# A new issue order for one fused attention and channel-mix kernel: the first loads in another sequence, every engine's list written anew

## The chip, the cores and the metric

The kernel runs on one core of a Trainium2 chip. A core has engines that each work through their own list of instructions in order: TensorE (PE, with its weight loads shown as PEld), VectorE (DVE), ScalarE (ACT), GpSimd (POOL) and SyncE (SP). SP, ACT and POOL also issue DMAs; the transfers run on 16 DMA engines that the queues share. An engine goes on to its next instruction only when the semaphores that this one waits for have been reached, so one late input holds everything behind it on the same engine. The metric is the device time in microseconds of one execution, the median of several.

## The reference

Two layers in a row. First a linear attention over 8 batches, 8 heads, 576 positions, head size 64:

```python
q_s = exp(q - max(q, -1));  q_s = q_s / sum(q_s, -1)        # softmax over the head size
k_s = exp(k - max(k, 2));   k_s = k_s / sum(k_s, 2)         # softmax over the positions
kv  = einsum('bhsd,bhse->bhde', k_s, v)
x   = einsum('bhsd,bhde->bhse', q_s, kv)                    # then (B, S, H*D) = (8, 576, 512)
```

Then a channel mix with weights `w_k` (512 x 1024), `w_v` (1024 x 512) and `w_r` (512 x 512):

```python
x_prev = x shifted by one position, zero at the start of each batch
xk = mu_k * x + (1 - mu_k) * x_prev
xr = mu_r * x + (1 - mu_r) * x_prev
out = sigmoid(xr @ w_r) * (relu(xk @ w_k) ** 2 @ w_v)
```

## The kernel before

The kernel has no loops on the chip. `graph` (from L187) makes a list of named operations with what each must follow and which buffers it takes and gives back; `Plan.ordered` (L159) then walks through the string `ORDER` (L48 to L125) and emits them in that order. A word of `ORDER` is `name:places`: the operation, and the numbers of the buffers that its new slots get. `ACT!load00q0` puts a load on ACT's queue in place of its usual one. Each operation has one engine, so the string fixes five lists, one for each engine; between engines only the data and the buffers order the work. Buffer numbers are shown in the profile as letters: `raw` 0 to 10 are raw_a to raw_k, `th` 0 to 6 are th_a to th_g, `mm` 0 to 3 are the PSUM banks mm_a to mm_d, and two pairs of banks att_a and att_b.

**Attention.** Work goes by pairs of a batch b and a group g of four heads (16 pairs, tag `bg`). `loadbgq`, `loadbgk`, `loadbgv` (L211) fetch q, k and v of a pair into raw buffers; batch 0 goes by SP and ACT and, for v, by POOL, and everything else by POOL's queue, 288 KB a piece for batches 0 and 1 (two pieces a tensor, last digit 0 or 1) and 576 KB after that. On POOL's queue stand also the weights: `wk00`, `wk01`, `wk10`, `wk11` (wk_aa, wk_ab, wk_ba, wk_bb, 256 KB each as written), `wr` (512 KB), `wv0` to `wv3`. ACT makes `expq`, `expk` (L337) and `cast` (v to bf16, L343); DVE makes `rsum`, `rrec`, `scale` (L352 to L361). On PE, `TKV`, or a joint block `B` or `M`, transposes q and multiplies k and v (L376, L406); a `B` or `M` block also holds the product of q and kv of an earlier pair (L545), which needs that pair's `qt` (ACT copy, L384) and `w` (DVE, L423). Then ACT copies the result out of PSUM (`xb`, `xs`, L553 and L557) and DVE makes the two mixes with the neighbouring position: `edge`, `diff`, `sc`, `mix` (L566 to L580). `mixbg0` feeds xk, `mixbg1` feeds xr.

**Channel mix.** The 4608 rows are cut into ten units u (512 rows, every fifth 256; unit 0 is 512 rows of batch 0, unit 2 reaches into batches 1 and 2). For each unit: eight groups `kuf` of four matmuls 128x512 (L673), each followed by `relu` on ACT (L660) and a square `sq` on DVE (L664); for each tile m of 128 rows `rum`, four matmuls with `wr` (L709), and a tanh `thum` on ACT (L714); then `vum0` and `vum1`, eight matmuls (L729), and `oum` on DVE (L735), which multiplies tanh and result inside the th buffer. Two stores `stum` (L745, first half, and `stum.2`, second half; 128 KB each) bring it out, on SP's queue.

Three uses of buffers matter below:

- A bank mm that a `k` took is free after its `relu`, one that an `r` took after its `th`, one that a `v` took after its `o`.
- A th buffer is taken by a `th` (ACT writes it) and free again when both stores of the tile that had it before have landed.
- A raw buffer is free when the `exp` or `cast` that reads it is done; the load that takes it next stands on POOL's queue.

At the start PE runs 27 `fill` matmuls on a constant, whose results nobody reads.

Of the kernel before, what the change touches and what calls it, by code (L numbers as in the profile page):

```python
# [60 lines left out]
load11v0:9 relu01:0 X001:0.3 k06:1 x0010 load11v1 wv0 expq110:0 wv1 x0111 k04:0 x0011 expk100
sq01 wv2 rrec101 scale101 TKV10:1 rsum110:3 rz10:2 w10:0 relu06:2 sq00 expq111 sq06 k05:2
relu04:0 k07:3 qt10:2 relu07:1 relu05:2 r00:1 r01:0 r03:3 rsum111 rrec110 rrec111 expk111:0
expk110 r02:2 sq05 wv3 scale111:0 cast110:1 sq07 scale110 cast111 B11:0.1 rz11:0 w11:1
# [14 lines left out]
load51q0:10 TKV30:1 rsum310:3 rrec310 relu24:0 v111 rz30:0 st13.2 k23:1 load41k0:0 cast310:2
expk400:2 sq24:0 o11 w30:1 sc2111:1 load41q0:2 k27:0 sc2110 o12 relu23:2 k20:3 k26:2 qt30:2  # L80
cast400:0 relu27:1 k21:1 scale310:1 mix211 B31:0.1 st13 sq23 relu21:0 mix201 sq27 k22:0 rz31:1
sq21 relu20:2 xb30:1 relu22:1 st03 w31:2 st11.2 st11 r23:1 xs30 rsum400:0 sq20 rrec400 sq22
th23:6 qt31:3 scale400:2 r22:3 edge30 th22:3 relu26:0 r30:0 diff30:0 sq26 sc3011:0 sc3010 k25:1
B40:1.0 v220:3 relu25:2 xb31:0 xs31 v200:2 th30:4 sc3001:1 v230:1 sq25 load61k0:1 load50q0:9
sc3000 edge31 expk410:0 v231 cast510:1 mix300 diff31:1 sc3100:2 sc3101 rz40:2 v201 cast410:2
expq410:2 load61v0:4 o23 v221 st01 w40:0 mix310 k41:0 r21:1 st12 o20 o22 st22.2 relu41:1
expq510:1 k40:2 v210:0 rsum410:1 rrec410 k42:3 load71q0:0 th21:0 sq41:1 st23 load50v0:5 relu40:0
relu42:2 k46:1 sq40 relu46:1 sc3111:1 qt40:1 st22 k37:2 expq500:0 scale410:0 st20.2 k33:3 k44:1
v211 rsum510:2 sq46 relu37:0 sq42 sc3110 expk510:1 B41:0.1 mix301 sq37:0 k34:2 relu44:1
load50k0:7 rrec510 rz41:0 o21 load60q0:2 relu33:2 mix311 w41:1 k45:1 k43:3 expk500:2 sq33 sq44  # L90
rsum500:3 relu43:0 xs40:1 relu45:2 k30:0 sq45 sq43 relu34:1 xb40 st20 k47:3 rrec500 relu47:2
scale500:1 st10 edge40 r33:1 th33:3 sq47 r31:2 diff40:0 st12.2 scale510:2 st10.2 k31:3 th31:2
relu30:0 load71k0:10 cast500:0 st23.2 r41:1 v410:2 k35:0 v411 sc4011:2 load60v0:9 expq600:2
load71v0:3 load61q0:7 relu31:2 th41:5 rsum600:0 o41 r40:3 sq31 sc4010 qt41:0 th40:1 load70k0:5
k36:1 sq30 relu35:2 mix401 sc4000:0 rrec600 qt50:2 sq34 relu36:0 M5:1.1 st41.2 k32:0 cast600:2
relu32:1 r32:1 st41 rz51:1 rz50:2 sc4001 sq35 xb41:0 w50:2 w51:0 sq32 v400:0 xs41 mix400
cast610:0 th32:6 sq36 edge41 expk600:0 cast710:1 qt51:3 diff41:1 v401 v320:2 sc4110:1 v300:3
v321 sc4101:2 sc4100 v301 mix410 sc4111 o32 k51:1 st21.2 expk610:1 o30 k57:2 mix411 v330:3 v331
expk710:2 relu51:2 expq610:0 relu57:1 scale600:0 o33 v310:1 st33.2 o40 expq710:1 rsum610:1
rrec610 v311 expq700:2 st30.2 o31 M6:1.0.1 k54:0 rz61:0 rz60:2 st21 w61:1 sq57:1 k53:1 sq51  # L100
xb50:1 relu54:0 xs50 edge50 relu53:1 k52:0 relu52:2 k55:1 diff50:0 sq54 w60:0 qt60:1 relu55:0
r50:0 sq52 xs51:0 k50:1 rsum700:3 scale610:1 k56:2 relu50:2 r53:3 sq50 rrec700 sq53 th50:5 xb51
edge51 sc5001:0 sc5000 mix500 sc5011:2 diff51:1 r51:1 sq55 r52:0 th53:0 relu56:2 v500:3 sq56
v530:2 sc5100:1 st40.2 st30 v531 expk700:0 st32.2 sc5010 sc5101 mix510 st32 th51:4 th52:6 v520:1
v501 k60:0 o53 relu60:1 scale700:2 k61:2 relu61:0 qt61:0 st31.2 o50 sc5110:0 rsum710:2 st31
sq60:0 k65:0 sc5111 k63:3 load70v0:2 cast700:0 st53.2 qt70:2 relu63:2 mix501 sq61 v521 o52 sq63
M7:1.0.1 k62:1 rz70:1 rz71:0 relu65:1 k66:0 w71:2 w70:0 relu62:0 xb61:1 sq62 xs61 mix511 edge61
relu66:2 rrec710 sq66 xs60:0 diff61:0 v510:1 st50.2 sc6101:1 v511 xb60 k67:0 k64:2 relu67:0
relu64:2 edge60 sq67 o51 sq64 r61:3 r63:0 v610:2 th61:2 st33 sq65 diff60:1 r60:1 st52.2 sc6001:2
th60:3 st40 st52 scale710:0 qt71:3 sc6100 sc6000 th63:1 mix600 sc6010:0 sc6111:2 v600:3 v611  # L110
v601 o60 st60 r62:1 v620:0 sc6110 st60.2 mix610 th62:6 k76:3 st53 sc6011 o61 k71:1 relu71:0
mix601 v621 o62 sq71:1 st51 k77:2 k75:1 relu75:2 sq75 k72:0 relu77:1 sq77 relu72:0 sq72 k73:1
k70:2 relu73:2 v630:0 st62 relu76:1 mix611 r72:1 relu70:0 th72:3 M8:1.1.0 v631 xs70:0 xs71:1
xb71 xb70 k74:1 sq76 sq70 r73:2 r71:3 th71:0 relu74:1 sq73 o63 edge70 edge71 diff70:0 diff71:1
# [796 lines left out]
```

## Time and profile before

| | |
|---|---|
| median of 3 runs | 194.69 us (194.67 to 194.73) |
| the profiled execution: its own time | 195.4 us |
| its span, first to last instruction | 193.6 us |
| around the span (195.4 - 193.6) | 1.8 us |
| profiled execution against the median | 0.7 us longer |
| mean granted TensorE clock | 0.995 |
| HBM read and written | 33.56 MB and 9.44 MB |

How to read it: the page first gives each engine's busy time, then the span in 40 slices of 4.84 us, where a digit is the busy share in tenths. Further views are the timeline (start, duration, instruction), the same by stretches of time, the DMA issues with their time from issue to landing, and the chain of work that ended last. Rows of SP's and ACT's queues (SPq, ACTq) and of POOL's DMA instructions give the time of the issue, not of the transfer. On an engine that is never idle the next instruction starts a little before the row of the last one ends, so that the cost of an instruction in a row of such is the distance of two starts, a little below its duration.

### The profile page before, as it was taken

The page shows a single profiled execution, that of the slowest core. Times are in us where ns is not written, and L with a number is a line of the kernel's source. Part 1 is how long each engine was busy: PE and PEld are TensorE (multiplying, and loading weights), DVE is VectorE, ACT ScalarE, POOL GpSimd, SP SyncE. Part 2 cuts the span into 40 slices and gives each one's busy share as a digit, 9 for nine tenths or more (in the row PEclk, how much of TensorE's full clock was granted, in tenths as well). Part 3 has the DMA queues.
Part 4 walks back from the last instruction along what each step waited for, and adds up shares of the span by engine and source line. Part 5 has one row for each costly group of instructions (what it writes and reads, how often), then busy time and mean ns, then how long its engine had stood idle before and what let it go on. Part 6 is the DMA issues. An engine that isn't in the chain of part 4 may idle for free.

```text
span 193.6 us, 4674 instructions
## 1 busy us (share of the span) xinstructions
PE 184.6 (95%) x1830; PEld 89.6 (46%) x1830; DVE 154.6 (80%) x368; ACT 138.8 (72%) x226; POOL 41.3 (21%) x65
## 2 busy tenths in 40 slices
PE   7698889999999999999999999999999999999991
PEld 2263344444545544655454544454444445554450
DVE  1788965999999999999999899997986494661521
ACT  3688899899999999899999878258425742357010
POOL 8346457453415402421200000000000000000000
PEclk9999999999999999999999999999999999999997
DMA  5999999999999997999990294253065003720085
GB/s 187 311 314 283 298 329 247 404 390 416 398 393 390 406 412 268 317 359 413 284 290 3 50 201 83 62 123 78 0 136 116 3 0 81 166 51 5 11 204 164
DMA packets 23614, 41.86 MB, mean 216 GB/s; under 512 B 9372, under 2 KB 12712, under 8 KB 23592
## 3 DMA queue, kind: packets, MB, share of 16 engines
q0 software_dynamic: 9392, 27.99, 43.3%
...
HBM read 33.56 MB, written 9.44 MB: 222 GB/s over the span
## 4 chain that ended last, share of the span: by engine, by line
PE 84%; DMA 11%; POOL 2%; issue 0%; DVE 0%; POOLq 0%
PE mm_a L729 9%; PE mm_a L673 9%; PE mm_b L673 9%; PE mm_d L729 8%; PE mm_c L729 8%; PE mm_b L729 7%; DMA wk_ab<-in_moe_w_k_dram 6%; PE mm_c L673 6%; PE mm_b L709 6%; PE mm_d L673 5%; DMA wr<-in_moe_w_r_dram 5%; PE mm_d L709 4%; PE mm_a L709 4%; PE mm_c L709 3%; PE att_b L545 1%; PE att_a L545 1%
## 5 line engine op out<-in xcount | busy, mean ns | idle before, releaser
L729 PEld LDWEIGHTS <-k_a 128*128 128x128 bf16 x152 | 14.6, 98 | 15.6 <-issue 0.5
L729 PEld LDWEIGHTS <-k_b 128*128 128x128 bf16 x144 | 13.9, 98 | 16.4 <-issue 0.2
L709 PEld LDWEIGHTS <-xr 128*128 128x128 bf16 x144 | 13.7, 98 | 16.6 <-DMA wr<-in_moe_w_r_dram 0.6
L709 PE MATMUL mm_b<-wr,xr 128*128 128x512 bf16 x48 | 12.5, 379 | 0.1
L673 PEld LDWEIGHTS <-wk_aa 128*128 128x128 bf16 x80 | 7.5, 98 | 8.7 <-issue 1.3
L673 PEld LDWEIGHTS <-wk_bb 128*128 128x128 bf16 x80 | 7.8, 98 | 7.7 <-DMA wk_bb<-in_moe_w_k_dram 0.2
L673 PEld LDWEIGHTS <-wk_ab 128*128 128x128 bf16 x80 | 7.7, 98 | 7.7 <-DMA wk_ab<-in_moe_w_k_dram 0.2
L673 PEld LDWEIGHTS <-wk_ba 128*128 128x128 bf16 x80 | 7.5, 98 | 8.2 <-issue 1.1
L709 PE MATMUL mm_d<-wr,xr 128*128 128x512 bf16 x36 | 9.2, 379 | 0.0
L664 DVE TENSOR_TENSOR k_b<-rel_b 128x512 bf16<-128x512 bf16 (+1 forms) x15 | 5.7, 381 | 4.4 <-ACT rel_b L660 4.2
L709 PE MATMUL mm_a<-wr,xr 128*128 128x512 bf16 x32 | 8.2, 379 | 0.0
L660 ACT ACTIVATE rel_a<-mm_b 128x512 bf16<-128x512 f32 (+1 forms) x8 | 4.7, 583 | 4.4 <-PE mm_b L673 2.3
L664 DVE TENSOR_TENSOR k_a<-rel_c 128x512 bf16<-128x512 bf16 (+1 forms) x14 | 5.6, 399 | 2.4 <-ACT rel_c L660 2.3
L660 ACT ACTIVATE rel_c<-mm_b 128x512 bf16<-128x512 f32 (+1 forms) x9 | 5.3, 590 | 3.0 <-PE mm_b L673 3.0
L673 PE MATMUL mm_b<-xk,wk_ab 128*128 128x512 bf16 x24 | 7.3, 379 | 0.0
L660 ACT ACTIVATE rel_b<-mm_a 128x512 bf16<-128x512 f32 (+1 forms) x7 | 4.2, 602 | 4.2 <-PE mm_a L673 4.2
L709 PE MATMUL mm_c<-wr,xr 128*128 128x512 bf16 x28 | 7.2, 379 | 0.0
L673 PE MATMUL mm_b<-xk,wk_aa 128*128 128x512 bf16 x24 | 7.2, 380 | 0.0
L664 DVE TENSOR_TENSOR k_a<-rel_a 128x512 bf16<-128x512 bf16 (+1 forms) x16 | 6.1, 384 | 1.2 <-ACT rel_a L660 1.2
L673 PE MATMUL mm_a<-xk,wk_ba 128*128 128x512 bf16 (+1 forms) x24 | 6.9, 370 | 0.0
L673 PE MATMUL mm_a<-xk,wk_bb 128*128 128x512 bf16 (+1 forms) x24 | 6.9, 370 | 0.0
L664 DVE TENSOR_TENSOR k_b<-rel_c 128x512 bf16<-128x512 bf16 (+1 forms) x14 | 5.4, 385 | 1.7 <-ACT rel_c L660 1.3
...
## 6 DMA issues: line engine op xcount, KB each, us to landing
raw_a<-in_q_dram POOLq DMA_DIRECT2D x3, 576.0 KB, 8.9
raw_c<-in_q_dram POOLq DMA_DIRECT2D x3, 576.0 KB, 9.7
raw_e<-in_v_dram POOLq DMA_DIRECT2D x3, 576.0 KB, 11.6
out_dram<-th_g SPq DMA_DIRECT2D x13, 128.0 KB, 2.4
out_dram<-th_d SPq DMA_DIRECT2D x12, 128.0 KB, 5.0
out_dram<-th_b SPq DMA_DIRECT2D x10, 128.0 KB, 4.2
out_dram<-th_a SPq DMA_DIRECT2D x10, 128.0 KB, 2.3
raw_b<-in_k_dram POOLq DMA_DIRECT2D x2, 576.0 KB, 10.9
```

The source lines that it names most:

```text
L545: kn.nc.tensor.matmul(kn.half(slot, u)[two[r], to:to + n], lhsT=kn.ws[w.index][two[u], r, :], rhs=x_columns(r, u, at, n), start=True, stop ...
L660: kn.nc.scalar.activation(out=kn.rels[rel.index][:, 0:n], in_=kn.bank(kf)[:, 0:n], func=ACT.Relu, scale=HALF_ROOT)
L664: kn.nc.vector.tensor_tensor(out=kn.k2s[k2.index][:, fc, 0:n], in0=kn.rels[rel.index][:, 0:n], in1=kn.rels[rel.index][:, 0:n], op=ALU.mult)
L673: kn.nc.tensor.matmul(kn.bank(kf)[:, 0:n], lhsT=kn.wk[fc // 4][ct % 2][:, ct // 2, (fc % 4) * 128: (fc % 4) * 128 + 128], rhs=kn.xs[0][:, ...
L709: kn.nc.tensor.matmul(kn.bank(rps), lhsT=kn.xs[1][:, ct, c:c + 128], rhs=kn.wr[:, ct, :], start=(ct == 0), stop=(ct == CT - 1))
L729: kn.nc.tensor.matmul(kn.bank(vps)[:, 0:width], lhsT=kn.k2s[k2.index][:, ft, 128 * m:128 * m + 128], rhs=wv_of(ft)[:, part], start=(ft == ...
```

## The change

Only `ORDER` differs. The set of operations (970 words) is the same, and so is every instruction's shape; the order and some buffer numbers change: 71 of the 76 lines are replaced by 70. PE's list is equal up to `fill.21 T01`; ACT's up to `x0000`, DVE's up to `kvn00`. The core of the diff:

```diff
 ACT!load00q0:0 zero ident load00q1 ACT!load00k0:1 load01q1:2 ACT!load01q0 rows load00v consts
-warm load00k1 load01v late load01k0:3 load10v1:4 wk00 load10q0:5 expq001:0 expq000 load10q1
-rsum001:0 ACT!load01k1 rsum000 wk01 expq011:1 rrec001 load10k1:6 rrec000 rsum011:1 fill:1
+warm load00k1 load01v late load01k0:3 load10q0:4 wk00 load10q1 expq001:0 expq000 load11q0:5
+rsum001:0 ACT!load01k1 rsum000 wk01 expq011:1 rrec001 load10k0:6 rrec000 rsum011:1 fill:1
...
-expk011 KV011 Z01 load10v0 wk11 qt01:1 rz01:1 edge01 kvn01:1 x0000 load11q0:7 load10k0 mu:2
+expk010:1 fill.19:3 fill.20:1 fill.21:1 T01:3 wk11 kvn00:0 edge00 wp000:0 fill.22:0 X000:1.0
+KV010:2 expk011 KV011 Z01 load10k1 wp001 qt01:1 x0001 load10v0:7 X001:0.3 load10v1 x0000 edge01
...
-load20v0:10 load20q0:0 load30q0:2 th01:0 load20k0:1 th02:1 v010:0 sq04 v000:2 th00:2 v030:1
+scale111 load30q0:10 cast110:1 expk110:0 load20v0:0 expk111 cast111 B11:1.0 rz11:0 load20q0:2
+sq04 w11:1 th03:0 th02:1 load20k0:1 sq05 th00:2 load21q0:3 v030:1 v010:0 xb10:0 v000:2 v031 xs10
...
-o00 st00.2 sc1101 mix1100 mix1101 v023 load30k0:8 o01 load40k0:9 k11:2 st03.2 k11.2 k11.3
...
-v100:1 scale300:0 th13:6 st01.2 th20:2 X21:0.1 xs21:1 xb21 sc2010:2 v120:2 expk300:0 th10:1
...
+load41v0:3 sq14 edge20 rrec300 qt21:1 scale300:0 expk300:0 r11:1 v120:0 th12:6 X21:1.0 v121
+cast400:1 v131 diff20:0 v100:2 v101 xb21:1 sc2011:2 xs21 st03 o12 o13 th11:1 sc2001:1 cast310:2
+edge21 cast300:0 v110:0 sc2000 diff21:1 sc2101:0 sc2100 st13 v111 mix200 o11 sc2010 expq310:2
+st11 st00.2 st00 expk310:1 r20:3 expq400:0 TKV30:1 load40k0:4 mix210 rz30:0 mix201 load41q0:6
+load60q0:8 o10 st10.2 k24:1 k21:0 load51k0:0 load70v0:5 k20:2 rsum310:3 st10 st13.2 st12.2 w30:1
+load71v0:7 rrec310 relu21:2 relu24:1 sq24:0 scale310:1 th20:2 load50v0:9 k23:0 k27:1 sc2111:1
+relu20:0 expk400:2 qt30:2 k25:3 sc2110 sq21 sq20 rsum400:0 k26:2 B31:0.1 relu26:1 relu25:2 k22:2
...
```

Taken apart by engine, the stretches that the prediction uses are these (before above, after below):

```
POOL  load00v load01v load10v1 wk00 load10q0 load10q1 wk01 load10k1 wk10 load10v0 wk11 load11q0 load10k0 load11q1 wr load11k1 load11k0 load11v0 load11v1 wv0 ..
      load00v load01v load10q0 wk00 load10q1 load11q0 wk01 load10k0 wk10 wk11 load10k1 load10v0 load10v1 load11q1 wr load11v0 load11k0 load11k1 load11v1 wv0 ..
POOL  .. wv3 load20v load20q load30q load20k load21q load21k load21v load60k load30v load30k load40k load31q load40q load31k load31v ..
      .. wv3 load30q load20v load20q load20k load21q load21k load21v load30v load31v load31q load30k load40q load40v load41k load31k ..
PE    .. X011 k01.2 X001 k06 k04 TKV10 k05 k07 r00 r01 r03 r02 B11 ..
      .. k02.2 X011 k07 k05 k06 k04 TKV10 r03 r02 r00 r01 B11 ..
PE    .. v110 k24 TKV30 v111 k23 k27 k20 k26 k21 B31 ..                (r20 earlier, after B21)
      .. v110 v111 r20 TKV30 k24 k21 k20 k23 k27 k25 k26 B31 ..
ACT   .. qt21 th13 th20 xs21 xb21 expk300 th10 cast300 expq310 expq400 expk310 relu24 cast310 expk400 relu23 qt30 ..
      .. qt21 expk300 th12 cast400 xb21 xs21 th11 cast310 cast300 expq310 expk310 expq400 relu21 relu24 th20 relu20 expk400 qt30 ..
SP    .. st00.2 st03.2 st00 st02.2 st02 st01.2 st13.2 st13 st03 st11.2 st11 st01 st12 ..
      .. st02 st02.2 st03 st13 st11 st00.2 st00 st10.2 st10 st13.2 st12.2 st01.2 st12 ..
DVE   edge10 diff10 sc1000 sc1001 sc1010 mix100 edge11 sc1011 diff110 diff111 o03 ..
      edge10 diff10 sc1000 sc1010 sc1001 sc1011 edge11 mix100 diff111 o01 diff110 sc1101 sc1100 sc1111 mix1100 mix1101 o03 ..
```

In both lists `th00` and `th20` have th buffer 2 (th_c), and in the new one `r20` and `k25` have bank 3 (mm_d), one after the other.

More of the change, by code (lines that the diff above doesn't have):

```diff
@@ L61 @@
[L61 to L64, printed above, removed]
-load20v0:10 load20q0:0 load30q0:2 th01:0 load20k0:1 th02:1 v010:0 sq04 v000:2 th00:2 v030:1
-xb10:0 v001 v031 xs10 v011 edge10 diff10:0 sc1000:0 sc1001 load21q0:3 qt11:3 th03:3 X11:1.0
@@ L67 @@
-xs11:1 xb111 v032 v002 load21k0:5 xb110 load21v0:4 v033 v020:3 v012 sc1010:1 mix100 edge11
-cast200:2 v003 v013 v021 sc1011 diff110:1 diff111 load60k0:6 load30v0:7 v022 o03 k13:1 sc1100:2
-o00 st00.2 sc1101 mix1100 mix1101 v023 load30k0:8 o01 load40k0:9 k11:2 st03.2 k11.2 k11.3
-sc1110:0 expq200:1 load31q0:10 expq300:2 o02 mix101 k13.2 sc1111 relu11:2 k15:0 sq11:1 rsum200:0
-k13.3 load40q0:0 k10:3 mix111 k10.2 expk200:1 k10.3 k17:2 relu15:1 k12:0 rrec200 k12.2 relu13:0
-sq15 expq210:0 k12.3 r12:1 relu10:2 load31k0:2 relu17:1 expk210:2 scale200:1 k16:3 st00
@@ L73 @@
-load31v0:1 sq13 rsum210:1 TKV20:0 load51k0:3 sq17 rz20:1 relu12:0 cast210:0 rrec210 relu16:1
-w20:2 r13:2 qt20:1 r11:0 st02.2 st02 scale210:2 k14:3 sq10 th11:4 relu14:2 sq12 th12:5 rsum300:2
-B21:1.0 r20:0 xs20:0 rz21:2 xb20 load51v0:5 w21:0 qt21:0 rrec300 sq14 edge20 sq16 diff20:0 r10:3
-v100:1 scale300:0 th13:6 st01.2 th20:2 X21:0.1 xs21:1 xb21 sc2010:2 v120:2 expk300:0 th10:1
-sc2000:1 edge21 sc2001 diff21:1 v130:0 cast300:1 sc2100:0 expq310:1 v131 v101 load40v0:4 sc2101
-mix200 expq400:0 expk310:1 o13 mix210 v110:3 v121 o10 sc2011 load70q0:8 load41v0:7 k24:0
@@ L79 @@
[L79 to L114, printed above, removed]
@@ new lines @@
+rz01:1 kvn01:1 wp010:1 mu:0 x0010 x0011 k01:1 X010:1.0 expq101:2 mucopy wp011 x0101 expq100
+x0100 rsum100:2 expk100:2 k00:2 k02:3 k03:0 k03.2 k01.2 relu01:0 rsum101 relu03:1 k00.2 load11q1
+wr rrec100 load11v0:8 sq01:0 scale100:2 load11k0:9 rrec101 sq03 k02.2 X011:0.1 x0111 relu00:2
+x0110 expq110:0 rsum110:3 k07:1 k05:0 load11k1 k06:2 sq00 relu02:0 expk101 cast100:0 cast101
+relu07:1 k04:3 scale101 sq07 TKV10:0 rz10:2 sq02 relu05:2 relu06:1 load11v1 expq111 wv0 wv1
+w10:0 r03:1 r02:0 wv2 r00:2 wv3 relu04:0 rrec110 scale110:0 rsum111 qt10:2 r01:3 rrec111 sq06
@@ new lines @@
+scale111 load30q0:10 cast110:1 expk110:0 load20v0:0 expk111 cast111 B11:1.0 rz11:0 load20q0:2
+sq04 w11:1 th03:0 th02:1 load20k0:1 sq05 th00:2 load21q0:3 v030:1 v010:0 xb10:0 v000:2 v031 xs10
+edge10 diff10:0 sc1000:0 sc1010:1 sc1001 v001 load21k0:4 v011 qt11:3 sc1011 X11:0.1 xs11:1
+th01:3 edge11 xb111 mix100 v012 load21v0:6 v013 load30v0:7 v002 v003 v020:3 xb110 diff111:1 o01
+diff110 sc1101:2 v032 expq300:1 load31v0:5 load31q0:9 sc1100 load30k0:8 v033 v021 v022
+load40q0:10 sc1111:0 k13:0 v023 mix1100 k13.2 mix1101 o03 k10:1 k13.3 o00 k12:2 cast200:2
@@ new lines @@
+expq200:2 k12.2 mix101 o02 load40v0:0 relu13:1 k10.2 load41k0:2 k10.3 rsum200:0 sq13:1 expk200:1
+k16:0 k12.3 k17:3 sc1110 relu10:0 rrec200 sq10 relu16:2 k14:1 k15:0 scale200:1 expq210:0
+relu17:1 mix111 relu14:0 sq16 k11:3 k11.2 expk210:2 rsum210:1 k11.3 relu11:2 sq11 TKV20:1
+load31k0:1 r13:1 rz20:1 cast210:0 rrec210 r10:3 w20:2 relu12:2 scale210:2 sq12 qt20:0 rsum300:2
+r12:2 th10:4 th13:5 st02 B21:0.1 v130:3 st02.2 relu15:2 rz21:2 sq15 w21:0 xb20:0 xs20 sq17
+load41v0:3 sq14 edge20 rrec300 qt21:1 scale300:0 expk300:0 r11:1 v120:0 th12:6 X21:1.0 v121
@@ new lines @@
+xs30:0 mix211 rz31:1 relu27:0 sq26 sq25 xb30 relu23:1 rrec400 w31:2 scale400:2 edge30 sq23 r22:3
+qt31:3 diff30:0 sq27 th22:4 relu22:2 st01.2 r23:1 th23:5 r30:0 B40:1.0 load61k0:1 xs31:1
+load50q0:10 load51q0:4 st12 xb31 r21:3 sq22 sc3000:0 th21:6 expk410:0 expq410:1 sc3001 expk510:1
+v230:2 v231 rz40:2 mix300 st03.2 v200:1 load51v0:2 edge31 diff31:1 th30:0 v220:3 sc3100:2 sc3101
+v201 o23 w40:0 load71q0:6 expq500:2 st11.2 mix310 k40:2 k46:0 relu46:1 relu40:0 rsum410:1 v221
+o20 sc3111:1 k41:0 sq46:1 relu41:2 sq40 k47:1 k42:2 relu47:1 sc3110 rrec410 o22 k36:0 k45:1
```

50 lines of the change are left out of this document (36 added, 14 removed).

## The prediction

> **What bounds the kernel now.** First the page: busy shares and slices.
>
> ```profile
> PE 184.6 (95%) x1830; PEld 89.6 (46%) x1830; DVE 154.6 (80%) x368; ACT 138.8 (72%) x226; POOL 41.3 (21%) x65
> ...
> PE   7698889999999999999999999999999999999991
> ```
>
> PE is full from its sixth slice of 4.84 us to the end, so the end is the time at which PE may start without gaps, plus its fixed work, plus any hole made in it later. Then the busy time by stretches:
>
> ```profile
> 20.00:25.00 5.00, 3.77 (x60) 1.68 (x60) 4.58 (x10) 4.29 (x9) 2.82 (x5) 1.00 1.15 303
> ...
> 35.00:60.00 25.00, 24.97 (x248) 11.47 (x245) 24.93 (x54) 23.49 (x33) 9.75 (x15) 1.00 1.04 399
> 60.00:75.00 15.00, 15.00 (x271) 7.55 (x270) 14.93 (x34) 15.00 (x23) 4.14 (x6) 1.00 1.04 403
> ...
> 100.00:130.00 30.00, 30.00 (x304) 14.07 (x303) 28.67 (x64) 22.62 (x36) 0.00 (x0) 1.00 0.43 93
> ```
>
> The second number of a row is PE's busy time, then PEld, DVE, ACT and POOL. From 35 to 75 us PE, DVE, ACT and the DMA engines (share 1.04) are all full at once. A wait on any of them there has no cover. After 100 us only PE is. Third, the chain of work that ended last, at its head:
>
> ```profile
> 5.35 12.36 DMA wk_ab<-in_moe_w_k_dram
> ...
> 18.00 9.29 DMA wr<-in_moe_w_r_dram
> ...
> 27.33 1.04 PE mm_b L709 x4
> ```
>
> The gapless part starts when `wr` has landed, at 18.00 + 9.29 = 27.29.
>
> **The first loads.** `wr` is the 15th load of POOL in both lists, and the same bytes stand ahead of it: four wk, two v of batch 0, eight pieces of pairs 10 and 11. Its issue followed the landing of the 7th (`wk01`, 5.35 + 12.36 = 17.71), which is the 7th again. So I take its landing as unchanged, 27.3. PE has the same groups ahead of the first `r` as before (`k04` to `k07` and `TKV10` among them), only with `TKV10` last; they need no more than before, and what PE saves of its holes (5.00 - 3.77 = 1.23 us between 20 and 25 us) is paid back by a longer wait for `wr`. This part: 0, bounds -0.3 (the wait for `wr` was already short) to +0.3.
>
> **Two small waits.** Cost of the new DVE order from 34.69:
>
> ```profile
> 34.69 0.84 DVE L575 TENSOR_SCALAR xm_a<-xd_a,mu 128x576 bf16<-128x576 bf16 x2
> 35.45 0.36 DVE L575 TENSOR_SCALAR xm_b<-xd_a,mu 128x576 bf16<-128x576 bf16 x1
> 35.72 0.75 DVE L580 TENSOR_TENSOR xk<-xm_a,xb_a 128x1152 bf16<-128x1152 bf16 x1
> 36.39 0.18 DVE L566 COPY xb_b<-xb_b 128x126 bf16<-128x126 bf16 x1
> 36.49 0.36 DVE L575 TENSOR_SCALAR xm_b<-xd_a,mu 128x576 bf16<-128x576 bf16 x1
> 36.77 0.81 DVE L570 TENSOR_TENSOR xd_b<-xb_b 128x576 bf16<-128x576 bf16 x2
> 37.51 0.67 DVE L735 SCALAR_TENSOR_TENSOR th_d<-th_d,mm_b 128x512 f32<-128x512 f32 x1
> 38.11 0.35 DVE L575 TENSOR_SCALAR xm_c<-xd_b,mu 128x576 bf16<-128x576 bf16 x1
> ...
> 39.27 0.81 DVE L580 TENSOR_TENSOR xk<-xm_c,xb_b 128x576 bf16<-128x576 bf16 x2
> 40.00 0.67 DVE L735 SCALAR_TENSOR_TENSOR th_a<-th_a,mm_a 128x512 f32<-128x512 f32 x1
> ```
>
> By the distances of starts, `o03` (the reader of mm_b) now has ahead of it four `sc` (0.76 + 0.27 + 0.28), `edge11` 0.10, `mix100` 0.67, two `diff` 0.74, `o01` 0.60, three `sc` 0.84 and two half mixes 0.73: it starts at 34.69 + 4.99 = 39.68 and ends at 40.35. `k10`, which takes mm_b, comes on PE right behind `k13 v023 k13.2`:
>
> ```profile
> 39.00 0.59 PE L673 MATMUL mm_b<-xk,wk_aa 128*128 128x512 bf16 x2
> ...
> 39.86 0.59 PE L673 MATMUL mm_c<-xk,wk_aa 128*128 128x512 bf16 x2
> ```
>
> that is at 39.86, where `k11` came before, plus one matmul, 0.22 (two take 39.86 - 39.00 less `v023`'s two, 0.43): 40.08. A wait of 0.3.
>
> Second, ACT now has `cast400` between `qt21` and `xb21`. Its tensor is the 13th load behind `wv3`; before, the 13th was this one into raw_a:
>
> ```profile
> 43.27 0.72 POOL L211 DMA_DIRECT2D raw_a<-in_q_dram  x1 [0.78 <-ACT rel_b L660]
> ```
>
> ```profile
> raw_a<-in_q_dram POOLq DMA_DIRECT2D x1, 576.0 KB, 13.0
> ...
> out_dram<-th_c SPq DMA_DIRECT2D x2, 128.0 KB, 5.8
> out_dram<-th_d SPq DMA_DIRECT2D x2, 128.0 KB, 8.4
> out_dram<-th_b SPq DMA_DIRECT2D x2, 128.0 KB, 8.7
> ...
> out_dram<-th_g SPq DMA_DIRECT2D x2, 128.0 KB, 7.8
> ```
>
> These are issues between 38 and 70 us, the last number the time to landing: 43.27 + 13.0 = 56.3, or half a microsecond less, as two stores fewer are out by then. ACT's rows:
>
> ```profile
> 53.66 0.66 ACT L714 ACTIVATE th_g<-mm_c 128x512 f32<-128x512 f32 x1
> ...
> 57.22 1.24 ACT L343 CAST vv_b<-raw_h 128x1152 bf16<-128x1152 f32 x1
> 58.26 1.25 ACT L337 ACTIVATE eq_b<-raw_k 128x1152 bf16<-128x1152 f32 x1
> 59.33 1.24 ACT L337 ACTIVATE eq_a<-raw_a 128x1152 bf16<-128x1152 f32 x1
> ...
> 64.02 0.68 ACT L660 ACTIVATE rel_c<-mm_b 128x512 bf16<-128x512 f32 x1
> 64.49 1.21 ACT L384 COPY qt_c<-att_b 128x1152 bf16<-128x1152 bf16 x1
> ```
>
> `qt21` ended as the first of these began; then come `expk300` (an `exp` or a `cast` costs 1.04 to 1.07) and `th12` (as a `relu`, 0.47): ACT gets to `cast400` at 55.2 and waits 0.5 to 1.1. So `xb21` starts at 56.7 to 57.4 and is out 1.1 later. Behind it DVE has in its new list `edge21`, three `sc`, `diff21`, `mix200`, `o11`, `mix210`, 3.8 us by rows of their kind above, so that `mix210` ends at 61.6 to 62.3. `k24` needs it and PE would reach it at 61.3 (worked out below) + 0.3: a wait of 0 to 0.7, and I take 0.6 as nearer to the 56.3 that a row gives. Together +0.9.
>
> **The store and the tanh.** This decides the forecast. Before, `st00` went out at 40 us. Now SP has `st13 st11 st00.2 st00`, and SP waits at `st11` for `o11`. `th20` takes the same th_c that `th00` had, so ACT must wait until `st00` has landed, and everything behind `th20` on ACT waits too. How long does a store take? Over the whole run:
>
> ```profile
> out_dram<-th_g SPq DMA_DIRECT2D x13, 128.0 KB, 2.4
> ```
>
> The median is 2.4 us, but the rows from 38 to 70 us, while POOL's loads fill the DMA engines, say 5.8 to 8.7. I take the loaded rows, since `st00` falls among the loads; with 2.4 it would be home before ACT asks (first rival). The Trainium skill ("DMA: Bandwidth & Descriptors", section on the anatomy of one DMA) fits one DMA on GpSimd's path as about 2.0 us plus bytes over 436 GB/s, an estimate of 2.3 us for 128 KB: the 2.4 agrees with it, the loaded rows do not, and by it the sum would be the first rival's.
>
> Issue: PE's list ahead of `v111` lacks `r20`, `k24` and `TKV30` that were there before, 2.6 us:
>
> ```profile
> 60.54 0.44 PE L376 MATMUL att_b<-ident,qs_a 64*128 64x64 bf16 x18
> ...
> 61.32 0.60 PE L729 MATMUL mm_d<-wv_c,k_b 128*128 128x512 bf16 x2
> ...
> 64.78 0.59 PE L673 MATMUL mm_c<-xk,wk_ba 128*128 128x512 bf16 x2
> ...
> 66.60 0.22 PE L545 MATMUL att_a<-qt_c,w_b 64*64 64x64 bf16 x4
> ```
>
> So `v111` starts at 58.7 (and `k24`, behind it, `r20` and `TKV30`, at 61.3) and ends 1.04 later (a group of four, as at 27.33) at 59.7, `o11` (0.67) at 60.4 at the earliest, at 61.2 where the late `xb21` holds DVE; I take 60.9. Three issues follow at the pace of these rows, the third 1.15 behind the first:
>
> ```profile
> 58.95 1.11 SPq L745 DMA_DIRECT2D out_dram<-th_g  x2
> 60.10 0.60 SPq L745 DMA_DIRECT2D out_dram<-th_d  x1
> ```
>
> `st00` goes at 62.1. The loads in flight then are as many as at 58.95 before. I take 7.9 us, between th_g's 7.8 and the 8.4 of the third store of that batch: landed at 70.0. ACT would stand at `th20` near 65 (53.66 plus seven `exp` and `cast` of 1.05, two `th` and two `relu` of 0.47, some 1.0 for `xb` and `xs`, and the wait for `cast400`). It waits about 5 us. PE meets this first at `k25`: it takes mm_d, which `th20` frees. `k25` has one group more ahead of it than `k26` had at 64.78 (`k21`), so it would come at 65.6 and waits until 70.5. Next late is `B31`, whose joint product needs `qt30`, four places behind `th20` on ACT: 70.0 + 0.47 + 0.47 + 1.07 + 1.21 = 73.2. Without waits `B31` comes at 66.60 + 0.86 (`k25` is now ahead of it) = 67.46. **PE loses 73.2 - 67.5 = 5.8 us**; the two small waits are inside this, as they delay what had to wait anyway. Everything behind shifts with PE; DVE and ACT, full until 100 us before, then have 5 us of slack, so no further hole follows, and PE's work behind `B31` is the same set.
>
> Bounds: with `o11` at 60.4 and 5.8 us for the store, landed at 67.4, PE loses 3.2; with 61.2 and 8.7, landed at 71.1, it loses 6.9. The profiled execution would go from 195.4 to 201.2; the median of the runs is 0.7 below it: **200.5**, own range 197.9 to 201.6.
>
> **The rivals.** *The store is home in time* (13%): the DMA engines serve it among the loads as among none, 2.4 us from 62.1, landed at 64.5 and so before ACT stands at `th20`; for it the 2.4 and the spread of the loaded rows down to 5.8, against it that all of these are above the 2.9 us that there are. Then the two small waits are left, +0.9: 195.6 (194.9 to 196.4). *Nothing is felt* (7%): these are covered too, `cast400`'s load landing before 55.2 and `o03` done by 40.1; PE's work being the same, 194.7. *The head gains* (8%, faster): if `wr` lands earlier, PE, with its work ahead of `wr` done sooner, could begin the `r` groups sooner by up to the 1.23 us of holes between 20 and 25 us, and the end would be 193.5. It decides from a landing of `wr` before 26.9 on and needs the store in time as well. Against it is the equal count of bytes ahead of `wr`.
>
> **How the numbers follow.** Forecast 72%, rivals 13, 7 and 8%. About 0.2%, 0.4 us, is what a measurement of this kernel tells from no change. Slower: 72 + 13 = 85%; within it 7%; faster 8%. The range of 8 in 10 takes the forecast's own and the first rival's, since the unknown latency of one store lies between them: 195.2 to 201.7; below it lie the last two rivals.
>
> **What would show it.** Right: in the new profile ACT idles about 5 us ahead of a tanh into th_c near 65 to 70 us, ended by the DMA out_dram<-th_c; PE has a hole near 66 at mm_d and one near 72 at qt_c; the store row for th_c tells 6 to 9 us; `wr` lands at 27.3 and PE's first L709 starts there. Wrong: ACT full across 60 to 75 us, or a first L709 before 26.9. The waits at mm_b near 40 and at `cast400` near 55 show or refute the two small terms.

## The result and the profile after

| | before | after |
|---|---|---|
| median | 194.68 us (194.56 to 195.26, 6 runs) | 202.5 us (201.39 to 203.4, 6 runs) |
| ratio, 95% interval | 1 | 1.0398 [1.0377, 1.0419] |
| the profiled execution | 195.4 us, span 193.6 us | 202.41 us, span 200.6 us |
| mean granted TensorE clock, profiled | 0.995 | 0.989 |

The kernel became 7.8 us slower. In the new kernel the lines of the code stand one lower: the tanh is L713, `k` L672, `r` L708, `v` L728, the store L744.

The page of the changed kernel, busy shares and slices (PE, then the clock that PE was granted):

```profile
PE 187.1 (93%) x1830; PEld 89.9 (45%) x1830; DVE 153.4 (76%) x368; ACT 139.4 (69%) x226; POOL 41.3 (21%) x65
...
PE   7999969999999099999989999999999999999992
...
PEclk9999999999999969999999999999999999999999
```

Before, PE's digits were 9 from the seventh slice on. Now the sixth slice has a 6, by a wait of 1.55 us for `wr`; there is a 0 in the 14th slice (65 to 70 us), and in the next slice the clock's digit falls to 6. A small dent, an 8, follows in the 21st slice. ACT's and PE's rows at the hole (start, duration, instruction; in brackets the idle time ahead and what ended it):

```profile
63.40 0.59 ACT L659 ACTIVATE rel_b<-mm_b 128x512 bf16<-128x512 f32 x1
69.94 0.60 ACT L713 ACTIVATE th_c<-mm_d 128x512 f32<-128x512 f32 x1 [5.95 <-DMA out_dram<-th_c]
...
71.96 1.12 ACT L383 COPY qt_c<-att_b 128x1152 bf16<-128x1152 bf16 x1
```

```profile
64.41 0.59 PE L672 MATMUL mm_b<-xk,wk_ba 128*128 128x512 bf16 x2
64.84 0.59 PE L672 MATMUL mm_b<-xk,wk_bb 128*128 128x512 bf16 x2
70.59 1.01 PE L672 MATMUL mm_d<-xk,wk_ba 128*128 128x512 bf16 x2 [5.15 <-ACT th_c L713]
71.40 1.06 PE L672 MATMUL mm_d<-xk,wk_bb 128*128 128x512 bf16 x2
72.25 1.06 PE L672 MATMUL mm_c<-xk,wk_ba 128*128 128x512 bf16 x2
73.10 0.77 PE L672 MATMUL mm_c<-xk,wk_bb 128*128 128x512 bf16 x2
73.80 0.22 PE L544 MATMUL att_a<-qt_c,w_b 64*64 64x64 bf16 x4
```

ACT stands 5.95 us ahead of the tanh into th_c until a store has landed, and PE 5.15 us ahead of `k25` until that tanh has freed mm_d. The same two matmuls of a `k` that take 0.43 us from start to start ahead of the hole take 0.81 to 0.85 behind it. The view by stretches (length, busy time of PE, PEld, DVE, ACT and POOL, granted clock, DMA share, GB/s) gives the clock:

```profile
70.00:71.00 1.00, 0.41 (x2) 0.13 (x2) 0.00 (x0) 1.00 (x3) 0.00 (x0) 0.52 1.02 408
71.00:72.00 1.00, 1.00 (x4) 0.41 (x3) 0.94 (x2) 1.00 (x3) 0.00 (x0) 0.50 1.06 420
72.00:73.00 1.00, 1.00 (x4) 0.29 (x2) 1.00 (x2) 1.00 (x2) 0.63 (x1) 0.50 1.03 410
73.00:74.00 1.00, 1.00 (x11) 0.32 (x13) 0.41 (x1) 0.17 (x2) 0.10 (x1) 0.78 1.04 408
74.00:75.00 1.00, 1.00 (x81) 0.78 (x70) 0.00 (x0) 1.00 (x3) 0.00 (x0) 1.00 1.05 399
```

From the end of the hole on PE ran at half its clock for some 3 us. The dent in the 21st slice, from the waits of ACT and of PE between 76 and 112 us:

```profile
ACT ek_c L336 <- DMA raw_i<-in_k_dram: 1.3, 1, 1.3
...
PE mm_d L708 <- ACT rel_a L659: 0.4, 1, 0.4
```

That is `expk500`, which waits for the load of k of (5,0), and through it `r31`.

### The profile page after: what moved, and what is told of

It is laid out like the page before. It is cut to its first block, busy times and chain, and to the rows that moved or that the text cites. A ratio compares the mean times of both kernels' runs of the same rounds, so it can differ in the third digit from the quotient of the medians.

```text
span 200.6 us, 4679 instructions
## 1 busy us (share of the span) xinstructions
PE 187.1 (93%) x1830; PEld 89.9 (45%) x1830; DVE 153.4 (76%) x368; ACT 139.4 (69%) x226; POOL 41.3 (21%) x65
## 4 chain that ended last, share of the span: by engine, by line
PE 50%; DMA 20%; issue 15%; POOL 6%; ACT 4%; DVE 2%; POOLq 0%; ACTq 0%
PE mm_d L728 6%; DMA wk_ab<-in_moe_w_k_dram 6%; DMA raw_a<-in_v_dram 6%; PE mm_b L728 5%; PE mm_c L728 5%; PE mm_c L672 5%; PE mm_a L672 4%; PE mm_b L672 4%; PE mm_a L728 4%; DMA wr<-in_moe_w_r_dram 4%; PE mm_b L708 4%; PE mm_d L672 3%; PE mm_a L708 3%; DMA raw_i<-in_k_dram 3%; PE mm_c L708 2%
## 5 line engine op out<-in xcount | busy, mean ns | idle before, releaser
L708 PEld LDWEIGHTS <-xr 128*128 128x128 bf16 x144 | 13.8, 98 | 18.2 <-DMA wr<-in_moe_w_r_dram 1.7
L728 PEld LDWEIGHTS <-k_a 128*128 128x128 bf16 x152 | 14.7, 98 | 15.6 <-issue 0.2
L728 PEld LDWEIGHTS <-k_b 128*128 128x128 bf16 x144 | 13.9, 98 | 16.8 <-issue 0.2
L708 PE MATMUL mm_b<-wr,xr 128*128 128x512 bf16 x52 | 13.4, 380 | 1.5 <-DMA wr<-in_moe_w_r_dram 1.5
L672 PEld LDWEIGHTS <-wk_ba 128*128 128x128 bf16 x80 | 7.7, 99 | 13.0 <-issue 6.2
L672 PEld LDWEIGHTS <-wk_bb 128*128 128x128 bf16 x80 | 7.9, 100 | 8.8 <-issue 1.5
L672 PEld LDWEIGHTS <-wk_aa 128*128 128x128 bf16 x80 | 7.3, 97 | 9.4 <-issue 2.1
L672 PEld LDWEIGHTS <-wk_ab 128*128 128x128 bf16 x80 | 7.8, 98 | 7.8 <-DMA wk_ab<-in_moe_w_k_dram 0.3
L708 PE MATMUL mm_d<-wr,xr 128*128 128x512 bf16 x36 | 9.2, 379 | 0.4 <-ACT rel_a L659 0.4
L672 PE MATMUL mm_d<-xk,wk_ba 128*128 128x512 bf16 (+1 forms) x16 | 4.5, 368 | 5.1 <-ACT th_c L713 5.1
L659 ACT ACTIVATE rel_b<-mm_a 128x512 bf16<-128x512 f32 (+1 forms) x11 | 5.9, 541 | 4.3 <-PE mm_a L672 4.3
L663 DVE TENSOR_TENSOR k_a<-rel_a 128x512 bf16<-128x512 bf16 (+1 forms) x13 | 5.1, 396 | 4.8 <-ACT rel_a L659 4.8
L659 ACT ACTIVATE rel_c<-mm_a 128x512 bf16<-128x512 f32 (+1 forms) x10 | 5.5, 553 | 4.5 <-PE mm_a L672 4.4
L663 DVE TENSOR_TENSOR k_b<-rel_a 128x512 bf16<-128x512 bf16 (+1 forms) x14 | 5.4, 387 | 4.1 <-ACT rel_a L659 4.1
L708 PE MATMUL mm_a<-wr,xr 128*128 128x512 bf16 x32 | 8.2, 379 | 0.0
L672 PE MATMUL mm_a<-xk,wk_bb 128*128 128x512 bf16 (+1 forms) x28 | 7.7, 356 | 0.0
L672 PE MATMUL mm_a<-xk,wk_ba 128*128 128x512 bf16 (+1 forms) x28 | 7.7, 356 | 0.0
L351 DVE TENSOR_REDUCE rsum_a<-eq_a 128x9 f32<-128x576 bf16 (+1 forms) x4 | 4.1, 1046 | 3.8 <-ACT eq_a L336 3.8
L663 DVE TENSOR_TENSOR k_a<-rel_b 128x512 bf16<-128x512 bf16 (+1 forms) x14 | 5.2, 373 | 2.0 <-ACT rel_b L659 2.0
L659 ACT ACTIVATE rel_c<-mm_b 128x512 bf16<-128x512 f32 (+1 forms) x6 | 3.4, 568 | 4.8 <-PE mm_b L672 4.8
L672 PE MATMUL mm_c<-xk,wk_ab 128*128 128x512 bf16 (+1 forms) x24 | 6.7, 352 | 0.0
```

The lines of the kernel that those rows point to most:

```text
L351: return kn.nc.vector.reduce_sum(out=sums(kn.rsums, u), in_=kn.eqs[eq.index][:, :, u, :], axis=AX.X)
L659: kn.nc.scalar.activation(out=kn.rels[rel.index][:, 0:n], in_=kn.bank(kf)[:, 0:n], func=ACT.Relu, scale=HALF_ROOT)
L663: kn.nc.vector.tensor_tensor(out=kn.k2s[k2.index][:, fc, 0:n], in0=kn.rels[rel.index][:, 0:n], in1=kn.rels[rel.index][:, 0:n], op=ALU.mult)
L672: kn.nc.tensor.matmul(kn.bank(kf)[:, 0:n], lhsT=kn.wk[fc // 4][ct % 2][:, ct // 2, (fc % 4) * 128: (fc % 4) * 128 + 128], rhs=kn.xs[0][:, ...
L708: kn.nc.tensor.matmul(kn.bank(rps), lhsT=kn.xs[1][:, ct, c:c + 128], rhs=kn.wr[:, ct, :], start=(ct == 0), stop=(ct == CT - 1))
L728: kn.nc.tensor.matmul(kn.bank(vps)[:, 0:width], lhsT=kn.k2s[k2.index][:, ft, 128 * m:128 * m + 128], rhs=wv_of(ft)[:, part], start=(ft == ...
```

## The experiments

**The store alone, and its place.** In the changed kernel only the two halves of `st00` move on SP, first to the head of the row, then only past `st11`.

```diff
 SP (s1)  .. muload [+st00.2 +st00] st02 st02.2 st03 st13 st11 [-st00.2 -st00] st10.2 ..
 SP (s4)  .. muload st02 st02.2 st03 st13 [+st00.2 +st00] st11 [-st00.2 -st00] st10.2 ..
```

> The two halves of st00 are issued on SP as soon as o00 is done (about 42 us), ahead of the other stores of unit 1, instead of behind st13 and st11 (61 us); nothing else is moved. Theory (the late store of th_c is most of the loss): ACT's 6.0 us wait before th20 is gone, PE's hole of 5 us at k25 and the slow clock behind it too, and the time falls by 5.3 + 1.3 us from 202.5 to about 196 (195.3 to 197.0). Rival A (only the wait goes, the slow clock at 70 to 75 us has another cause): about 197.2. Rival B (the new order as a whole is late, and the store only the first place where it shows; B31 or a following unit then waits for something else): the time stays over 199.

> The changed kernel with st00's two halves between st13 and st11 on SP, so that they are issued behind st13 at about 57 us, 4.5 us earlier, among the same loads. Theory (latency 8.4 us as in the changed kernel): landed at about 65.2, th20 waits about 1 us instead of 6, and st11 goes 1.2 us later, at 61 or as before, with no one waiting for it; the time is about 197 (196.2 to 198). Rival (the wait for th_c isn't what holds the end): over 200.

Measured: 196.28 us (6 runs, ratio 1.007 [1.005, 1.0089]) and 196.1 us (5 runs, 1.0065 [1.0042, 1.0088]). The first lies within its theory's range, the second 0.1 us below its own; the medians fit none of the rivals. The stretch that held the hole, with `st00` at the head of the row:

```profile
65.00:70.00 5.00, 4.95 (x99) 2.54 (x99) 5.00 (x11) 4.75 (x9) 0.72 (x1) 1.00 1.04 406
```

The two issues of `st00`, first in the changed kernel, then behind `st13`; for the latter also ACT's wait and the time to landing that its view gives:

```profile
60.90 1.23 SPq L744 DMA_DIRECT2D out_dram<-th_c  x2
```

```profile
56.99 1.24 SPq L744 DMA_DIRECT2D out_dram<-th_c  x2
```

```profile
64.51 0.60 ACT L713 ACTIVATE th_c<-mm_d 128x512 f32<-128x512 f32 x1 [0.56 <-DMA out_dram<-th_c]
```

```profile
out_dram<-th_c SPq DMA_DIRECT2D x2, 128.0 KB, 6.2
```

With the store issued 3.9 us earlier, and under way for less time as well, ACT's wait is 0.56 us instead of 5.95, and 6.4 of the 7.8 us are back. So the late store of one buffer, and no general lateness of the new order, makes most of the loss.

**Why the store is late: the loads in flight.** The changed kernel with six loads held back until `rsum310`, the store left where it was.

```diff
-.. load41v0:3 .. load40k0:4 .. load41q0:6 load60q0:8 .. load51k0:0 load70v0:5 .. rsum310:3
+.. rsum310:3 load40k0^rsum310:4 load41v0:3 load41q0:6 load60q0:8 load51k0:0 load70v0:5
```

(`^rsum310` makes the load wait for that instruction on VectorE, and what stands behind it on POOL with it.)

> The changed kernel with the load of k of (4,0) and the five loads behind it held until rsum310 (about 63.5 us), so that the last load in flight when st00 is issued (61.5 us) is one that landed at 64.2; the place of the store on SP is as it was. Theory (the 8.4 us from issue to use are the store's packets behind the queued loads): the store lands about 3 us after its issue or right behind the last load, 64.5 to 66, th20 waits 0 to 2 us instead of 6, and the time is 196 to 199, if the later loads don't become late themselves. Rival (a store from this queue takes 6 to 8 us in itself): th20 still starts at 69 to 70 and the time is 202 to 203.

Measured: 202.8 us (4 runs, 1.0423 [1.0378, 1.0468]), the time that the rival named, but not by its mechanism. The issues of the two stores ahead of `st00`, with the time to landing, first in the changed kernel, then in this one, and ACT's rows in this one:

```profile
out_dram<-th_f SPq DMA_DIRECT2D x2, 128.0 KB, 5.7
out_dram<-th_b SPq DMA_DIRECT2D x2, 128.0 KB, 7.2
```

```profile
out_dram<-th_f SPq DMA_DIRECT2D x1, 128.0 KB, 2.2
out_dram<-th_b SPq DMA_DIRECT2D x1, 128.0 KB, 2.2
```

```profile
65.55 0.60 ACT L713 ACTIVATE th_c<-mm_d 128x512 f32<-128x512 f32 x1 [1.53 <-DMA out_dram<-th_c]
66.04 0.59 ACT L659 ACTIVATE rel_a<-mm_c 128x512 bf16<-128x512 f32 x1
68.91 1.16 ACT L336 ACTIVATE ek_c<-raw_e 128x1152 bf16<-128x1152 f32 x1 [2.28 <-DMA raw_e<-in_k_dram]
```

Both take 2.2 us when few loads or none run beside them. (POOL issues no load between 46.14 and 64.22 us here, and from 59 to 60 us the DMA share is 0.00; the load landing at 64.2 that the expectation counted on isn't there.) `th20` waits 1.5 us instead of 6. `st00` itself goes out at 61.6 and lets the tanh start at 65.55, after 4.0 us instead of 8.4: the loads are the larger part of its latency. The rest, above the 2.2 of the others, stays open; two stores go out just ahead of it, and the loads begin again at 64.22.

The time is not won, because the held load of k of (4,0) is now what ACT waits for, and with it `qt30` and `B31`:

```profile
PE att_a L544 <- ACT qt_c L383: 3.0, 1, 3.0
```

Another hole of 2.2 us follows on PE at 85 us. The bound of the expectation "if the later loads don't become late themselves" was broken, so this run gives the cause of the latency and no price.

**The slow clock.** The changed kernel with matmuls on a constant in the hole; nothing else moved (its code stands ten lines lower).

```diff
-.. k23:0 k27:1 sc2111:1
+.. k23:0 k27:1 heat:0 heat.2:0 [...] heat.23:0 sc2111:1
```

> The changed kernel with 23 added matmuls of 512 columns on a constant tile of zeros, in the order of TensorE between k27 and k25, where it stands idle for 5 us; nobody reads their result, and the store stays late. Theory (the granted clock falls because TensorE idled): th20 still waits 5 to 6 us for the store, k25 and k26 take 0.9 us again instead of 1.6, the granted clock from 70 to 75 us stays above 0.9, and the time falls by 0.6 to 1.3 us to about 201.4. Rival (the clock falls by a rhythm of its own or through the DMA traffic): k25 and k26 stay at 1.5 us and the time is 202.3 to 202.9.

Measured: 200.86 us (4 runs, 200.65 to 202.28; 1.0322 [1.0283, 1.0362]), 1.64 us less than the changed kernel. PE's rows:

```profile
65.26 5.13 PE L310 MATMUL att_a<-still 128*128 128x512 bf16 x23
70.50 0.59 PE L682 MATMUL mm_d<-xk,wk_ba 128*128 128x512 bf16 x2
70.92 0.59 PE L682 MATMUL mm_d<-xk,wk_bb 128*128 128x512 bf16 x2
...
73.04 0.22 PE L554 MATMUL att_a<-qt_c,w_b 64*64 64x64 bf16 x4 [0.66 <-ACT qt_c L393]
```

`k25` starts when it does in the changed kernel (70.50 against 70.59), at full speed (granted clock 1.00 from 70 to 73 us), and `B31` at 73.04 instead of 73.80. It waits only for `qt30`, as the prediction had it. So the clock fell because PE idled, and by the medians adding useless work makes the kernel faster. What the slow clock costs in the end stays open. Of the 0.76 us won at `B31` in the trace, 0.64 go again at `r31` (see below), and this execution took 202.28 us, the slowest of its four. The medians say 1.64, but the two sets of runs overlap. So it is 0.1 to 1.6.

**The late load of k of (5,0), and the rest.** On the kernel with `st00` behind `st13` first one pair of loads is swapped (s5); then `st00` goes right behind `st03`, and `cast400` behind `cast310`, as well (s6).

```diff
-.. load71k0:3 load50k0:8 .. load61v0:8
+.. load50k0:3 load71k0:8 .. load61v0:3
```

```diff
 SP   .. st02.2 st03 [+st00.2 +st00] st13 [-st00.2 -st00] st11 ..
 ACT  .. th12 [-cast400] xb21 xs21 th11 cast310 [+cast400] cast300 ..
```

> The kernel with st00 behind st13 (196.1 us), and in it the load of k of (5,0) ahead of that of (7,1) on POOL, into buffer 3 instead of 8, so that it is issued at about 83.5 us instead of 87.2; the loads of k of (7,1) and v of (6,1) swap buffers accordingly. Theory (expk500 is late by its load): ACT's wait of 1.8 us for raw_i at 91.8 us is gone, with it TensorE's 0.9 us at mm_d near 95, and the time falls by 0.8 to 1.0 us to about 195.2. Rival (TensorE's 0.9 us there is only the place where another lateness of the new order comes out): the wait moves, and the time stays at 196.0 to 196.3.

> The changed kernel with three moves: st00's halves right behind st03 on SP (issued near 43 us), the load of k of (5,0) early as above, and cast400 behind cast310 instead of ahead of xb21 on ACT. Theory (what is left of the loss beside the store is the sum of named waits: 0.6 us at qt_c by th20, 0.3 to 0.7 us at mm_b by mix210, 0.9 us at r31): 196.1 less 1.5 to 1.9 is 194.2 to 194.6, no slower than before (194.9). Rival (the new order has less slack everywhere, other waits come up where these go): 195.3 to 196.1, slower than before.

Measured: 195.54 us (10 runs, 1.0046 [1.0027, 1.0065]) and 195.11 us (12 runs, 1.0018 [0.9997, 1.0039]). Ahead of the first move the wait stands on ACT like this (kernel with `st00` behind `st13`):

```profile
ACT ek_c L336 <- DMA raw_i<-in_k_dram: 1.8, 1, 1.8
```

With it the row is gone, and the median falls by 0.56 us, some two thirds of what the theory named; the two sets of runs overlap. The second kernel is between what theory and rival named and can't be told from the kernel before. Of PE's waits over 0.2 us these are left in it:

```profile
PE mm_b L708 <- DMA wr<-in_moe_w_r_dram: 1.5, 1, 1.5
PE mm_b L300 <- DVE qt_d L247: 1.1, 1, 1.1
```

The second is among the fills at the start, and the kernel before has it too (1.1).

**The first loads.** The kernel with `st00` behind `st13`, and in it POOL's first loads in the order of the kernel before; and the kernel before once more.

```diff
-POOL load00v load01v load10q0 wk00 load10q1 load11q0 wk01 load10k0 wk10 wk11 load10k1 load10v0 load10v1 load11q1 wr load11v0 load11k0 load11k1 load11v1
+POOL load00v load01v load10v1 wk00 load10q0 load10q1 wk01 load10k1 wk10 load10v0 wk11 load11q0 load10k0 load11q1 wr load11k1 load11k0 load11v0 load11v1
```

> The kernel with st00 behind st13 (196.1 us), and in it the first loads of POOL in the order of the kernel before (v of (1,0) first, k before v of (1,1)), their buffers renumbered so that later loads wait for the same instructions; all other orders are the changed kernel's. Theory of the prediction (the order of the first loads is worth nothing, because wr is the 15th load either way): the first instruction that reads wr starts within 0.3 us of the 26.8 us of this family and the time is 195.8 to 196.4. Rival A (the order of the first loads brought the 0.5 us by which wr landed earlier): the first r at 27.3, time about 196.6. Rival B (the engines' orders fit only their own loads): TensorE waits 1 us or more more before 27 or 30 to 36 us, time over 197.

> The kernel before once more, for a second trace of its head. If the landing of wr at 27.3 us is fixed by the order of the loads, the first r starts at 27.2 to 27.4 again; if it wanders from run to run, it starts anywhere from 26.7 to 27.4.

Measured: 201.79 us (4 runs, 1.036 [1.0329, 1.0391]), 5.7 us more than with the new first loads: rival B, far beyond what I had expected. The one run of the kernel before took 195.34. ACT's and PE's rows:

```profile
17.91 0.62 ACT L504 CAST xk<-att_b 128x576 bf16<-128x576 f32 x1
23.29 0.68 ACT L336 ACTIVATE ek_c<-raw_g 128x576 bf16<-128x576 f32 x1 [4.76 <-DMA raw_g<-in_k_dram]
```

```profile
24.51 1.01 PE L672 MATMUL mm_b<-xk,wk_ba 128*128 128x512 bf16 x2 [3.43 <-ACT rel_a L659]
```

The new list of ACT has `expk100` ahead of the first `relu`s. In the new order of loads its half of k is the 8th load of POOL; in the old one it is the 13th, and everything behind `expk100` waits 4.76 us. The reverse (the new first loads under the old lists) wasn't tried. Of the head itself, the first `r` in the kernel before again, in the changed one, and in that of the next run (s8):

```profile
26.87 1.04 PE L709 MATMUL mm_b<-wr,xr 128*128 128x512 bf16 x4
```

```profile
26.78 1.04 PE L708 MATMUL mm_b<-wr,xr 128*128 128x512 bf16 x4 [1.55 <-DMA wr<-in_moe_w_r_dram]
```

```profile
25.95 1.04 PE L708 MATMUL mm_b<-wr,xr 128*128 128x512 bf16 x4 [0.68 <-ACT rel_b L659]
```

The kernel before starts it at 26.87 in this execution and at 27.33 in the first one. So most of the 0.55 us by which the changed kernel was earlier is within what this time wanders from one execution to another.

**Trying to win the head.** `wr` one place earlier in the kernel of 195.11 us (s8), with `o03` ahead of `mix1101` (s9), with `expq111` behind `relu04` as well (s11); and `o03` alone (s10).

```diff
 POOL  .. load10v1 [+wr] load11q1 [-wr] load11v0 ..          (s8, s9, s11)
 DVE   .. mix1100 [+o03] mix1101 [-o03] ..                   (s9, s10, s11)
 ACT   .. [-expq111] relu04 [+expq111] qt10 ..               (s11)
```

> The kernel with all three moves (195.1 us), and in it the load of wr one place earlier on POOL, ahead of the second half of q of (1,1) (288 KB) instead of behind it. Theory (the head is set by the place of wr in the row of loads: TensorE is done with its other work at 24.9 us and waits 1.5 us for wr): wr lands 0.7 to 0.9 us earlier, the first r starts at about 26.0 and the time falls by 0.5 to 0.9 us to 194.2 to 194.6. Rival (the half of q that now lands later, through expq111 on ACT and qt10, holds TensorE at B11 near 30 us): the time is 195.0 to 195.8.

> The kernel of the run before this one, and in it o03 ahead of mix1101 on VectorE instead of behind it. Theory (k10 waits 0.2 to 0.3 us for mm_b by o03, as the prediction put it): the time falls by 0.2 to 0.3 us below that of the run before. Rival (k13.3 waits for mix1101 in its place, or a later wait takes it up): less than 0.1 us.

> The kernel with all three moves (195.1 us), and in it o03 ahead of mix1101 on VectorE; wr stays where it was. Theory (k13.3, which waits 0.3 us behind k10, is followed at once): 0.2 to 0.3 us less, 194.8 to 194.9, level with the kernel before. Rival (the next wait takes it up): 195.0 to 195.2.

> The kernel with wr one place earlier and o03 moved (195.35 us), and in it expq111 behind relu04 on ACT instead of ahead of it. Theory (TensorE's 0.7 us at B11 near 30 us is ACT's wait for the half of q of (1,1), which holds back what stands behind it): ACT does relu04 in that wait, B11 starts 0.4 to 0.5 us earlier and the time is 194.8 to 195.0. Rival (scale111 and the transposes of B11 become the late ones): 195.3 or more.

Measured: 195.63 us (11 runs, 1.0032 [1.0014, 1.0051]), 195.35 (12 runs, 1.0026 [1.0008, 1.0044]), 195.05 (11 runs, 1.0017 [1.0008, 1.0026]) and 194.99 (11 runs, 1.0018 [1.0006, 1.0031]), beside 194.89 and 194.83 for the kernel before. PE's waits in s8, ACT's between 18 and 36 us in s8, and PE's between 20 and 60 us in s11:

```profile
PE att_b L405 <- ACT vv_b L342: 0.8, 1, 0.8
PE mm_b L708 <- ACT rel_b L659: 0.7, 1, 0.7
```

```profile
ACT eq_a L336 <- DMA raw_f<-in_q_dram: 0.8, 1, 0.8
```

```profile
PE mm_b L708 <- DMA wr<-in_moe_w_r_dram: 0.7, 1, 0.7
PE att_b L405 <- ACT vv_b L342: 0.3, 1, 0.3
```

In s8 `wr` is 0.9 us earlier at the first `r`, and the 0.8 us comes back at `B11`: ACT waits 0.8 us for the half of q that `wr` overtook. That is the rival. Moving ACT's wait behind `relu04` takes 0.36 us off, as the theory had it. `o03` shows 0.28 us in s9 and 0.06 in s10; the first is what was expected, the second isn't. None of these three is above what a measurement can tell. None of these kernels beats the kernel before; their intervals lie a little above 1.

## Why the prediction had the main wait right and was short by 2.0 us

**The main term stands.** All its links are in the trace: `st00` issued at 61.5 (predicted 62.1), home 8.4 us later at 69.94 (7.9, and 70.0), `k25` at 70.59 (70.5), `qt30` out at 73.1 (73.2). That the landing agrees to 0.1 us is luck: the issue was some 0.5 us early, as the first `r` was 0.55 us earlier than in the trace that it was worked out from, and the latency was 0.5 us longer. The runs with the store earlier show the cause; the run with the loads held shows that the loads are the larger part of the latency. One sign that was named is missing: PE has no hole near 72 us at qt_c, as it was still at `k26` with half its clock when `qt30` was out.

**What failed is one sentence: "so no further hole follows, and PE's work behind `B31` is the same set".** The set is the same, its duration isn't, and one hole does follow. On the profiled executions, 201.2 was predicted and 202.41 came:

- `B31` started at 73.80, not 73.2: +0.6. PE ran its first matmuls behind the hole at half clock. I counted the wait and not what the wait does to the clock. The Trainium skill ("TensorE: Matmul & The Clock Gate", part 1, on the clock gate) has this: PE falls to half rate after an idle window of about 3.4 us and is released after as long a busy one. The trace agrees, with 0.50 for some 3 us behind a gap of 5.15 us, and the added matmuls show that it is the idling.
- From `B31` to the end it took 202.41 - 73.80 = 128.6 us. Before it was 195.4 - 66.60 - 0.86 (`k25`, now ahead) = 127.9. So +0.7 behind `B31`. PE's rows have 0.54 of it: 0.40 ahead of `r31`, and 0.14 ahead of the next group into mm_b at 103.91, whose bank a tanh behind `expk500` freed late. The chain that ended last goes through the load that `expk500` waits for:

```profile
93.23 5.88 DMA raw_i<-in_k_dram
```

The two parts don't simply add up. `r31` in the changed kernel and in the one with the added matmuls:

```profile
101.88 1.02 PE L708 MATMUL mm_d<-wr,xr 128*128 128x512 bf16 x4 [0.40 <-ACT rel_a L659]
```

```profile
101.76 1.02 PE L718 MATMUL mm_d<-wr,xr 128*128 128x512 bf16 x4 [1.04 <-ACT rel_a L669]
```

In the second, `B31` came at 73.04, as forecast, at full clock; then `r31` waits 0.64 us longer and starts only 0.12 earlier, and the execution took 202.28, still 1.1 above the forecast. So in these two traces the late load of k of (5,0) is enough for what is missing, and hides nearly all of the slow clock. The prediction put every wait behind `B31` at nothing because DVE and ACT would have 5 us of slack there; what came was a wait of ACT for a load, and the prediction names no load behind `B31`.

**The step from the profiled execution to the median** took off 0.7, because the profiled execution of the kernel before was that much above its median. In the changed kernel both are equal (202.41 and 202.5). In the runs here profiled executions lay from 0.4 us below to 1.6 us above the medians of their kernels, so that 0.7 was no constant to carry over. Why they differ is not known.

Sum: 0.6 + 0.7 + 0.7 = 2.0, which is 202.5 - 200.5. The upper end of the range, 201.7, was made from the moment of `o11` and the latency of one store alone, so none of the three was in it.

**The smaller steps.** PE was full from the seventh slice on before, not from the sixth, which has an 8; nothing rests on it. The head: the first `r` at 26.78 is below the 26.9 that was named as a sign of being wrong, and beyond the bound of -0.3; but the kernel before has 26.87 in its second trace, so that this sign tells nothing. The saved holes were paid back by a wait for `wr`, 1.55 us, as forecast. So 0 stands within what the head wanders, though for the count of loads ahead of `wr` alone; that the new lists need the new first loads I had not seen. `k10`'s wait for `o03` was predicted as 0.3 and is in the trace:

```profile
39.87 0.59 PE L672 MATMUL mm_b<-xk,wk_aa 128*128 128x512 bf16 x2 [0.17 <-DVE th_a L734]
```

The row before it starts at 39.31 with one matmul of 0.22, so it is 0.34 by starts. `cast400` was to wait 0.5 to 1.1:

```profile
55.00 1.15 ACT L342 CAST vv_b<-raw_a 128x1152 bf16<-128x1152 f32 x1 [0.34 <-DMA raw_a<-in_v_dram]
```

It waited 0.34; the load landed at 55.0 (42.69 + 12.29) instead of 56.3. `k24` then stood 0.25 us for `mix210`, where 0.6 had been taken. The forecast took both as covered by the 5.8 us. For `cast400` that isn't shown, since its wait lies on the store's way: DVE idles 0.49 us until 57.26, when `xb21` lets `edge21` begin, works without a gap from there to `o11`, and `st11` and `st00` follow `o11`.

**By medians** the 7.8 us are: 6.4 for the store, with the slow clock that it brings; 0.56 for the load of k of (5,0) and 0.43 for the last waits at `th20` and `cast400`, both between sets of runs that overlap. What is left, 0.26 between 195.11 and the 194.85 of the kernel before in the same batch, is no more than a measurement can tell; the last 0.17 is between the two batches' kernels before (194.68 and 194.85).
